# Clustered attention and two dense layers on one core: half-tile PSUM buffers, casts on three engines, a new order

## The chip, the cores and the metric

One core of a Trainium2 chip runs the whole program. The metric is the device time of one execution in microseconds (us). TensorE is called PE below (PEld is its weight load), VectorE DVE, ScalarE ACT, GpSimd POOL and SyncE SP.

## The reference

```
# B, H, S, D = 2, 8, 768, 64; 16 clusters per head
q_assign, k_assign = argmax over the clusters of normalized q, k against normalized centroids
mask   = q_assign[..., :, None] == k_assign[..., None, :]
scores = where(mask, 0.125 * q @ k.T, -1e9)
attn   = exp(scores - max); attn /= sum; x = attn @ v        # 16 heads, (768, 64) each
x = x.transpose(0, 2, 1, 3).reshape(1536, 512)
h = x @ w_in                                                 # 512 -> 2048
x = where(h > 0, h, exp(min(h, 0)) - 1) @ w_out              # 2048 -> 512
out = ((x @ w_a) * (x @ w_b)) @ w_out2                       # 512 -> 1536 -> 512
```

## The kernel before

The program is a list of small operations, written out by hand in the string `ORDER`. A word such as `tr:6.3` calls the operation `tr` with the numbers 6 and 3. No scheduler moves anything: each engine gets its instructions in the order of the words and works them off in that order. Semaphore waits come from the tiles that the instructions share. Two instructions on different engines that touch the same bank of one PSUM tile wait for each other, whichever columns they touch.

**Attention.** The 16 heads go in 8 pairs (pair j holds heads 2j and 2j+1), with 6 tiles of 128 query rows per head, so 12 tiles per pair. For head g and tile t:
- `sc:g.t` (PE): scores into one of two `sc` buffers of two banks. `rm` (DVE) takes the row maximum, and `ex` (ACT) the exponential with its sum, into `pf`. `ex` frees the `sc` buffer.
- The probabilities are needed with keys on partitions, as two 16-bit parts. 30 of the 96 tiles take the way `hi` (cast), `lo` (POOL subtracts), `td` (a transposing DMA). The other 66 take `tr` (six PE transpositions of 128x128 into PSUM), `th` (ACT casts the 768 columns to 16 bits) and `tl` (DVE subtracts that from the 768 columns).
- `av:j.f.n` (PE): the product with v in three parts. `ra`, `rc`, `rx`, `rb`, `re` spread the reciprocals of the sums, `ev` (DVE) scales the result.

Once per pair, ahead of its scores, the clusters are found: `sm` (PE) gives similarities, `sv` copies them out of PSUM, `st` transposes them (PE), `m1` to `m5` are five DVE instructions on the transposed tile in PSUM, `oh` transposes the result back (PE), `ohs` (ACT) scales it, and `ohd` stores it by DMA into rows that the scores use. `lk`, `lq`, `ka1`, `ka2`, `qa`, `qb`, `kbd` load and split a head's k and q; `vs`, `v1`, `v2` do the same for v. At the start `vr` (ACT) takes the maxima of v, which `vtp`, `vtd`, `vbp`, `vbd` spread. `wm` is 8 small matmuls that keep PE busy and whose result nobody reads.

**PSUM in attention.** Four banks are the two `sc` buffers. One tile `places` has three banks, split into two slots of 768 columns, that is one and a half banks each, which `small` hands out in turn: transpositions, `st`, `oh`, `rb`, `vtp` and `vbp` use them. The middle bank belongs to both slots. The last bank is the tile `sums`: `av` and `sm` in its first 384 columns, `wm` in the rest.

**The dense layers** follow: `h`, `r1`, `r2`, `g`, `gh`, `gl`, `x2`, `xa` and `ab`, `bs`, `pr`, `ph`, `pl`, `o`, `oa`, each product as three matmuls of 512 columns, with the weights prepared by `wl` to `wq` (loads, ACT, DVE, POOL) some pieces ahead.

Of the kernel before, what the change touches and what calls it, by code (L numbers as in the profile page):

```python
# [69 lines left out]
m2:0 wm:29 vr:7 m3:0 wm:30 vr:8 wm:31 m4:0 wm:32 vr:9 m5:0 wm:33 vr:10 oh:0 vr:11 wm:34 ohs:0 wm:35  # L70
wm:36 vr:12 ohd:0 wm:37 ka1:2.2 vr:13 wm:38 vr:14 wm:39 ka2:2.1 vr:15 kbd:2 wm:40 vtp:0 qa:2.1 wm:41
vtd:0 wm:42 ka1:3.2 wm:43 wm:44 ka2:3.1 kbd:3 qa:3.1 vbp:0 wm:45 vbd:0 wm:46 wm:47 qb:2 wm:48 wa:1
sc:0.0 w0:1 sc:0.1 rm:0.0 vs:0 wm:49 vs:1 rm:0.1 ex:0.0 wm:50 wm:51 lk:4.0 w1:1 wm:52 lq:4.0 ex:0.1
w2:1 sc:0.2 w3:1 tr:0.0 wh:1 lk:5.0 w4:1 sc:1.0 th:0.0 ws:1 rm:0.2 tr:0.1 v1:0.1 rm:1.0 th:0.1 wm:53
wq:1 wm:54 tl:0.0 wm:55 ex:0.2 wm:56 v2:0.2 wl:2 tl:0.1 wm:57 ex:1.0 sc:1.1 vs:2 wm:58 qb:3 hi:0.2.1
sc:1.2 v1:1.1 rm:1.1 lo:0.2 tr:1.0 lq:5.0 v1:2.1 sm:1.0 rm:1.2 ex:1.1 v2:1.2 td:0.2 th:1.0 sc:0.3
vs:3 wa:2 tr:1.1 rm:0.3 v2:2.2 sv:1.0.1 wm:59 w0:2 th:1.1 sm:1.1 w1:2 ex:1.2 w2:2 w3:2 wh:2 sc:0.4
w4:2 sv:1.1.1 ws:2 tl:1.0 ra:0.0 ex:0.3 rm:0.4 st:1 wq:2 hi:1.2.1 tl:1.1 sc:0.5 ex:0.4 lo:1.2 wl:3
m1:1 tr:0.3 m2:1 qa:4.1 sc:1.3 rm:0.5 ka1:4.2 td:1.2 th:0.3 rc:0.0 ka2:4.1 ex:0.5 kbd:4 m3:1 m4:1
hi:0.5.1 sc:1.4 m5:1 rx:0.0 rm:1.3 wa:3 oh:1 lo:0.5 ohs:1 tl:0.3 ex:1.3 w0:3 ohd:1 tr:0.4 w1:3  # L80
rb:0.0 th:0.4 w2:3 sc:1.5 w3:3 wh:3 w4:3 td:0.5 re:0.0 ws:3 rm:1.4 av:0.0.0 qa:5.1 ex:1.4 tl:0.4
av:0.0.1 wq:3 rm:1.5 tr:1.3 v1:3.1 lk:6.0 ka1:5.2 sc:2.0 th:1.3 qb:4 kbd:5 av:0.0.2 ex:1.5 rm:2.0
ka2:5.1 lq:6.0 tr:1.4 ra:0.1 hi:1.5.1 sc:2.1 ev:0.0 tl:1.3 th:1.4 lo:1.5 ex:2.0 rm:2.1 v2:3.2 tl:1.4
td:1.5 ex:2.1 sc:2.2 lk:7.0 vs:4 tr:2.0 rm:2.2 sc:3.0 vs:5 th:2.0 rc:0.1 tr:2.1 rm:3.0 rx:0.1 ex:2.2
qb:5 th:2.1 sc:3.1 tl:2.0 ex:3.0 lq:7.0 sm:2.0 rm:3.1 hi:2.2.1 sc:3.2 tl:2.1 sv:2.0.1 lo:2.2 rb:0.1
ex:3.1 rm:3.2 av:0.1.0 re:0.1 td:2.2 ex:3.2 sc:2.3 av:0.1.1 rm:2.3 ra:1.0 hi:3.2.1 sc:2.4 rc:1.0
lo:3.2 tr:3.0 rm:2.4 av:0.1.2 th:3.0 rx:1.0 ex:2.3 tr:3.1 ev:0.1 tl:3.0 sm:2.1 th:3.1 td:3.2 ex:2.4
tl:3.1 sc:2.5 sv:2.1.1 sc:3.3 rm:2.5 ka1:6.2 qa:6.1 st:2 ka2:6.1 rm:3.3 kbd:6 ex:2.5 tr:2.3 m1:2
hi:2.5.1 m2:2 sc:3.4 th:2.3 m3:2 lo:2.5 m4:2 ex:3.3 av:1.0.0 m5:2 tl:2.3 v1:4.1 oh:2 v1:5.1 v2:4.2
sc:3.5 rm:3.4 ohs:2 tr:2.4 ka1:7.2 qa:7.1 rm:3.5 ohd:2 rb:1.0 ka2:7.1 th:2.4 av:1.0.1 re:1.0 tl:2.4  # L90
ex:3.4 av:1.0.2 v2:5.2 td:2.5 lk:8.0 tr:3.3 ex:3.5 ev:1.0 kbd:7 tr:3.4 qb:6 th:3.3 sc:4.0 qb:7
# [975 lines left out]
```

## Time and profile before

| | |
|---|---|
| median of 3 runs | 908.3 us (907.98 to 908.95) |
| profiled execution | 908.33 us |
| its span, first to last instruction | 906.5 us |
| mean granted clock of PE | 0.969 of full speed |
| busy, share of the span | PE 94%, DVE 66%, ACT 47%, POOL 37% |

The time holds 1.8 us that lie outside the span. The shares are averages over two stages that differ: attention, to about 350 us, and the dense layers after it.

### The profile page before, as it was taken

The numbers are of one execution on the slowest core, as the hardware profiler recorded it, in microseconds if no ns is written. First come the engines' busy times: TensorE is split into PE (matmuls) and PEld (weight loads), VectorE is DVE, ScalarE is ACT, GpSimd is POOL, SyncE is SP. The second block draws the span as 40 slices with busy tenths as digits, with TensorE's granted clock in tenths as the row PEclk, the third lists the DMA queues.
The fourth block names the chain that finished last, engine by engine and source line by source line (L and its number), as shares of the span: only waits on it lengthen the run. The fifth ranks groups of instructions, "written<-read, shape, count | busy, mean of one in ns | idle before, by whom it ended". The sixth has DMA issues, their size and how long they took to land.

```text
span 906.5 us, 12080 instructions
## 1 busy us (share of the span) xinstructions
PE 850.3 (94%) x4608; PEld 671.6 (74%) x4608; DVE 595.5 (66%) x791; ACT 428.8 (47%) x707; POOL 333.8 (37%) x274
## 2 busy tenths in 40 slices
PE   8878888798898789999999999999999999999997
PEld 7856665565565567888888888888888888888886
DVE  4567677666665778997767868898436772574222
ACT  4667686676766666526417416534122341232120
POOL 4455534526432333454334343445104441252000
PEclk9979999898987999999999999999999999999999
DMA  9345346254423222222222231222002230120102
GB/s 279 99 90 117 69 101 111 50 117 104 94 53 57 45 60 70 70 93 69 70 70 70 69 90 51 72 90 92 25 1 76 87 94 24 47 93 1 40 8 93
DMA packets 65754, 68.32 MB, mean 75 GB/s; under 512 B 49952, under 2 KB 49952, under 8 KB 65696
## 3 DMA queue, kind: packets, MB, share of 16 engines
q1 hardware_dynamic: 65392, 66.86, 27.7%
q10 hardware_dynamic: 304, 0.69, 0.3%
q8 instruction: 36, 0.59, 0.3%
q14 instruction: 22, 0.18, 0.1%
HBM read 48.27 MB, written 3.15 MB: 57 GB/s over the span
## 4 chain that ended last, share of the span: by engine, by line
PE 83%; DVE 8%; ACT 4%; issue 1%; ACTq 0%; DVEq 0%
PE ab L871 7%; PE ab L872 7%; PE ab L870 7%; PE places L673 6%; PE sc L623 6%; PE h L870 5%; PE h L871 5%; PE h L872 5%; PE x L870 5%; PE x L871 5%; PE x L872 5%; PE sums L730 4%; PE o L872 4%; PE o L870 4%; PE o L871 4%; DVE pt L682 4%
## 5 line engine op out<-in xcount | busy, mean ns | idle before, releaser
L631 DVE TENSOR_REDUCE nm<-sc 128x1 f32<-128x768 f32 x96 | 91.0, 952 | 35.2 <-PE sc L623 34.9
L642 ACT ACTIVATE pf<-sc,nm 128x768 f32<-128x768 f32 x96 | 86.5, 904 | 13.2 <-DVE nm L631 12.1
L682 DVE TENSOR_TENSOR pt<-places,pt 128x768 f16<-128x768 f32 x66 | 62.7, 953 | 29.5 <-ACT pt L677 12.4
L655 POOL TENSOR_TENSOR phl<-pf,phl 128x768 f16<-128x768 f32 x30 | 49.4, 1648 | 86.6 <-ACT phl L650 82.4
L677 ACT CAST pt<-places 128x768 f16<-128x768 f32 x66 | 52.4, 798 | 58.0 <-PE places L673 18.5
L673 PE MATMUL places<-identf,pf 128*128 128x128 f32 x396 | 62.9, 302 | 13.3 <-DVE pt L682 5.8
L972 ACT COPY t0ab<-ab 128x512 f32<-128x512 f32 x36 | 21.1, 586 | 110.6 <-PE ab L872 110.6
L977 DVE TENSOR_TENSOR t1ab<-ab,t0ab 128x512 f32<-128x512 f32 x36 | 24.9, 690 | 72.4 <-ACT t0ab L972 72.3
L623 PE MATMUL sc<-ka,qa 128*128 128x384 f32 x192 | 61.8, 405 | 10.9 <-ACT pf L642 10.6
L673 PEld LDWEIGHTS places<-identf,pf 128*128 128x128 f32 x396 | 48.2, 152 | 29.4 <-DVE pt L682 11.2
L730 PE MATMUL sums<-pt,v 128*64 128x384 f16 x576 | 55.0, 333 | 0.0
L623 PE MATMUL sc<-kb,qb 80*128 80x384 f32 x192 | 52.8, 358 | 0.0
L836 DVE SCALAR_TENSOR_TENSOR wg<-wraw,wg 128x512 f32<-128x512 uint32 x68 | 51.2, 754 | 2.0
L623 PEld LDWEIGHTS sc<-ka,qa 128*128 128x128 f32 x192 | 31.8, 204 | 26.4 <-ACT pf L642 18.0
L823 DVE SCALAR_TENSOR_TENSOR wf<-wraw,wg 128x512 int32<-128x512 int32 x68 | 47.0, 691 | 2.0
L806 ACT ACTIVATE wg<-wraw 128x512 f32<-128x512 f32 x68 | 45.3, 669 | 2.3 <-DMA wraw<-in_w_out_dram 2.2
L988 DVE TENSOR_TENSOR gl<-t1ab,gh 128x512 fp32r<-128x512 f32 x36 | 31.5, 874 | 19.9 <-ACT gh L983 19.7
L811 DVE TENSOR_SCALAR wg<-wg 128x512 f32<-128x512 f32 x68 | 44.0, 647 | 0.4
L730 PEld LDWEIGHTS <-v 128*64 128x64 f16 x576 | 29.7, 111 | 19.5 <-issue 7.9
L816 DVE TENSOR_SCALAR wg<-wg 128x512 int32<-128x512 int32 x68 | 40.7, 598 | 2.0
L926 DVE SCALAR_TENSOR_TENSOR t1h<-t0h,h 128x1024 f32<-128x1024 f32 x24 | 29.2, 1217 | 18.6 <-ACT t0h L921 18.6
L831 DVE TENSOR_SCALAR wg<-wf 128x512 int32<-128x512 int32 x68 | 29.0, 427 | 14.9 <-POOL wf L850 13.2
(378 smaller groups left out, 2352.5 us busy)
## 6 DMA issues: line engine op xcount, KB each, us to landing
wraw<-in_w_out_dram SPq DMA_DIRECT2D x28, 512.0 KB, 3.2
wraw<-in_w_in_dram SPq DMA_DIRECT2D x16, 512.0 KB, 3.6
wraw<-in_w_a_dram SPq DMA_DIRECT2D x12, 512.0 KB, 3.5
wraw<-in_w_b_dram SPq DMA_DIRECT2D x12, 512.0 KB, 3.5
rawq<-in_qt_dram SPq DMA_DIRECT2D x30, 192.0 KB, 4.1
acc<-in_v_dram SPq DMA_DIRECT2D x4, 768.0 KB, 10.7
rawk<-in_kt_dram SPq DMA_DIRECT2D x15, 192.0 KB, 3.7
kb<-ka SPq DMA_DIRECT2D x14, 192.0 KB, 3.2
```

Of the source, the lines that this page charges most:

```text
L623: nc.tensor.matmul(s[:, j, :HALF], a[:, qs], b[:, j * HALF : (j + 1) * HALF], start=i == 0, stop=i == 1,)
L631: nc.vector.reduce_max(out=nm, in_=st[g][f"sc{t}"][:, :, :HALF], axis=AX.XY, negate=True)
L642: nc.scalar.activation(pf.rearrange("p (a b) -> p a b", a=2), st[g].pop(f"sc{t}")[:, :, :HALF], AF.Exp, bias=st[g].pop(f"nm{t}"), accum_ou ...
L655: nc.gpsimd.tensor_sub(phl[:, S:], st[g].pop(f"pf{t}"), phl[:, :S])
L673: nc.tensor.transpose(tt[:, ks], pf[:, ks], identf)
L677: nc.scalar.copy(next(parts_of(g, t)), st[g][f"tt{t}"])
L682: nc.vector.tensor_sub(lo, st[g].pop(f"tt{t}"), hi)
L730: nc.tensor.matmul(pairs[j]["av"][x * 64 : (x + 1) * 64].rearrange("p (a q) -> p a q", a=3), st[2 * j + x][("v1", "v2")[vi]][:, kt_, :], s ...
L836: nc.vector.scalar_tensor_tensor(out=g, in0=raws.pop(n)[:, :, 0].bitcast(U32), scalar=2.0 ** -52, in1=g, op0=ALU.mult, op1=ALU.mult,)
L870: nc.tensor.matmul(ps, lhi, rhi, start=first, stop=False)
L871: nc.tensor.matmul(ps, lhi, rlo, start=False, stop=False)
L872: nc.tensor.matmul(ps, llo, rhi, start=False, stop=last)
```

## The change

- `places` and `sums` go. `small` now takes one of three buffers of one bank each (tag `tt`), for half tiles of transpositions and all the small products, `sm` among them. `av` has a bank of its own, which `wm` uses ahead of it.
- `tr`, `th` and `tl` work on half tiles of 384 columns: 132 of each, with three transpositions in a `tr`, where there were 66 with six.
- The result of `m5` and its transposition `oh` are bf16, with a bf16 identity (`ib` makes it).
- Casts and copies that were on one engine are shared out. `hi`: 30 on ACT become 14 on ACT and 16 on POOL. `th`: 66 on ACT become 126 halves on ACT and 6 on DVE. `v1`: 16 on ACT become 5 on DVE, 3 on ACT, 8 on POOL. `v2`: 5 of 16 go from POOL to DVE. `ka1`: 10 of 16 go from POOL to ACT. `qa`: 7 of 15 go from ACT to POOL and 1 to DVE. `re`: 4 of 16 and `sv`: 4 of 16 go from ACT to DVE.
- `ORDER` is a new list; the other operations are the same in number.

```diff
-    places = psumA.tile([P, 2 * S], F32, name="places")
-    nplace = [0]
-    sums = psumA.tile([P, 512], F32, name="sums")
-    def small(shape):
-        o = nplace[0] % 2 * S
-        nplace[0] += 1
-        t = places[: shape[0], o : o + int(np.prod(shape[1:]))]
...
+    def small(shape, name, dt=F32):
+        return take(psumA, "tt", shape, dt, name, 3)
...
-        ps = pairs[j]["sm", hf] = sums[:64, :HALF]
+        ps = pairs[j]["sm", hf] = small([64, HALF], f"sm_{j}_{hf}")
...
-        o = pairs[j]["op"] = small([64, S])
+        o = pairs[j]["op"] = small([64, S], f"op_{j}", BF16)
...
-        (nc.vector.tensor_copy, nc.scalar.copy)[e](phl[:, :S], st[g][f"pf{t}"])
+        (nc.vector.tensor_copy, nc.scalar.copy, nc.gpsimd.tensor_copy)[e](
+            phl[:, :S], st[g][f"pf{t}"]
+        )
...
-        for k in range(NT):
-            ks = slice(k * P, (k + 1) * P)
-            nc.tensor.transpose(tt[:, ks], pf[:, ks], identf)
+    def tr(g, t, u):
+        tt = st[g][f"tt{t}{u}"] = small([P, HALF], f"tt{t}{u}_{g}")
+        pf = st[g][f"pf{t}"]
+        for k in range(3):
+            o = u * HALF + k * P
+            nc.tensor.transpose(tt[:, k * P : (k + 1) * P], pf[:, o : o + P], identf)
...
-            pairs[j]["av"] = sums[:, :HALF]
+            pairs[j]["av"] = take(psumA, "av", [P, HALF], F32, f"av_{j}_{f}")
```

How the new list moves instructions is seen on each engine's own list.

**PE around the cluster step of pair 4, before.** `places` here is first the transposed similarities, then a tile of probabilities, then `oh`.

```order
L557 MATMUL places_82<-identf_88,sim_4_1948 128x64 x6
L623 MATMUL sc4_7_2121<-ka_7_1446,qa_7_1448 128x384 x2
L623 MATMUL sc4_7_2121<-kb_7_1504,qb_7_1521 128x384 x2
L673 MATMUL places_82<-identf_88,pf3_6_2054 128x128 x6
L598 MATMUL places_82<-identf_88,oht_4_2146 64x128 x6
```

The same place now: `tp_4` is the transposed similarities, `op_4` the result of `oh`, `rbp` that of `rb`, `tt30` and `tt31` two half tiles.

```order
L701 MATMUL tt30_6_2252<-identf_87,pf3_6_2223 128x128 x3
L701 MATMUL tt31_6_2259<-identf_87,pf3_6_2223 128x128 x3
L649 MATMUL sc3_7_2263<-ka_7_1586,qa_7_1590 128x384 x2
L649 MATMUL sc3_7_2263<-kb_7_1593,qb_7_1611 128x384 x2
L583 MATMUL tp_4_2273<-identf_87,sim_4_2113 128x64 x6
L741 MATMUL rbp_3_0_2285<-identf_87,rx_3_0_2249 128x128 x3
L649 MATMUL sc4_7_2295<-ka_7_1586,qa_7_1590 128x384 x2
L649 MATMUL sc4_7_2295<-kb_7_1593,qb_7_1611 128x384 x2
L649 MATMUL sc5_7_2313<-ka_7_1586,qa_7_1590 128x384 x2
L649 MATMUL sc5_7_2313<-kb_7_1593,qb_7_1611 128x384 x2
L624 LDWEIGHTS oht_4_2309
L624 MATMUL op_4_2323<-identb_82,oht_4_2309 64x128
```

The tile of probabilities stands ahead of the step instead of inside it, and `rb` and two score tiles stand between `st` and `oh`, where there were one score tile and the tile of probabilities.

**DVE at the same step, before.**

```order
L631 TENSOR_REDUCE nm3_7_2114<-sc3_7_2095 128x1
L570 TENSOR_REDUCE mx_4_2128<-places_82 128x24
L575 TENSOR_TENSOR places_82<-places_82,mx_4_2128 128x384
L580 TENSOR_TENSOR places_82<-places_82,desc_93 128x384
L584 TENSOR_REDUCE mx_4_2128<-places_82 128x24
L589 TENSOR_TENSOR oht_4_2146<-places_82,mx_4_2128 128x384
L682 TENSOR_TENSOR pt1_6_2142<-places_82,pt1_6_2142 128x768
L631 TENSOR_REDUCE nm4_7_2166<-sc4_7_2121 128x1
```

And now:

```order
L710 TENSOR_TENSOR pt1_6_2268<-tt30_6_2252,pt1_6_2268 128x384
L657 TENSOR_REDUCE nm3_7_2280<-sc3_7_2263 128x1
L596 TENSOR_REDUCE mx_4_2291<-tp_4_2273 128x24
L601 TENSOR_TENSOR tp_4_2273<-tp_4_2273,mx_4_2291 128x384
L606 TENSOR_TENSOR tp_4_2273<-tp_4_2273,desc_92 128x384
L610 TENSOR_REDUCE mx_4_2291<-tp_4_2273 128x24
L615 TENSOR_TENSOR oht_4_2309<-tp_4_2273,mx_4_2291 128x384
L710 TENSOR_TENSOR pt1_6_2268<-tt31_6_2259,pt1_6_2268 128x384
L657 TENSOR_REDUCE nm4_7_2321<-sc4_7_2295 128x1
```

The five instructions stay together in this pair; a `tl` on 384 columns stands on either side, where one on 768 stood behind them.

**ACT at the start, before.** `junk,vmax` are the maxima of v (`vr`), `sim_0` the two copies `sv` of pair 0, `ohs_0` its `ohs`.

```order
L549 COPY sim_0_396<-sums_83 64x384
L844 CAST w0h_348<-wf0_351 128x512
L403 ACTIVATE junk_110,vmax_107<-acc_66 128x384 x2
L549 COPY sim_0_396<-sums_83 64x384
L403 ACTIVATE junk_110,vmax_107<-acc_66 128x384 x10
L603 ACTIVATE ohs_0_540<-places_82,ohscale_95 64x768
L403 ACTIVATE junk_110,vmax_107<-acc_66 128x384
L611 DMA kb_0_293<-ohs_0_540 16x768
L611 DMA kb_1_313<-ohs_0_540 16x768
L403 ACTIVATE junk_110,vmax_107<-acc_66 128x384 x3
```

And now:

```order
L519 CAST ka_0_314<-rawk_0_154 64x768
L427 ACTIVATE junk_110,vmax_107<-acc_66 128x384 x14
L629 ACTIVATE ohs_0_541<-op_0_526,ohscale_94 64x768
L836 ACTIVATE wg0_561<-wraw0_250 128x512
L637 DMA kb_0_296<-ohs_0_541 16x768
L637 DMA kb_1_209<-ohs_0_541 16x768
L427 ACTIVATE junk_110,vmax_107<-acc_66 128x384 x2
```

The two copies of similarities have left ACT, so nothing that PE computes stands ahead of the first 14 maxima. On PE `vbp` now stands behind the first two score tiles instead of ahead of them.

## Rows read from the trace of the kernel before

**Rows 1.** The page's slices: TensorE's granted clock, tenths, 40 slices of the span.

```profile
PEclk9979999898987999999999999999999999999999
```

**Rows 2.** Stretches: length, then busy us of PE, PEld, DVE, ACT, POOL; clock, DMA.

```profile
200.00:250.00 50.00, 40.90 (x277) 28.36 (x275) 34.79 (x45) 34.63 (x65) 24.73 (x21) 0.92 0.48 96
...
350.00:400.00 50.00, 50.00 (x220) 40.83 (x219) 45.91 (x53) 24.12 (x31) 20.25 (x13) 1.00 0.22 74
```

**Rows 3.** Timeline around pair 4's cluster step: start, duration, engine, line, [idle before <-releaser].

```profile
169.51 0.58 PE L557 MATMUL places<-identf,sim 64*128 64x64 f32 x6
...
171.69 0.87 PE L673 MATMUL places<-identf,pf 128*128 128x128 f32 x6 [0.64 <-DVE places L575]
...
172.61 0.57 DVE L580 TENSOR_TENSOR places<-places,desc 128x384 f32<-128x384 f32 x1 [0.97 <-PE places L673]
173.21 0.80 ACT L677 CAST pt<-places 128x768 f16<-128x768 f32 x1 [1.49 <-DVE places L580]
...
175.10 0.95 DVE L682 TENSOR_TENSOR pt<-places,pt 128x768 f16<-128x768 f32 x1
...
176.11 1.49 PE L598 MATMUL places<-identf,oht 128*64 128x128 f32 x6 [3.54 <-DVE pt L682]
...
178.68 1.54 PE L673 MATMUL places<-identf,pf 128*128 128x128 f32 x6
...
179.20 1.81 POOL L502 TENSOR_TENSOR ka<-rawk,ka 64x768 fp32r<-64x768 f32 x1
...
179.79 2.03 DVE L456 SCALAR_TENSOR_TENSOR qb<-rawq,qa 64x768 fp32r<-64x768 f32 x1
```

**Rows 4.** Stretches from `oh` to `oh`, and from the last to attention's end.

```profile
176.11:213.02 36.91, 31.79 (x209) 22.39 (x209) 25.45 (x32) 25.55 (x47) 16.69 (x14) 0.92 0.46 91
213.02:250.24 37.22, 32.05 (x209) 22.63 (x209) 25.44 (x32) 25.55 (x47) 16.68 (x14) 0.91 0.49 105
...
287.40:349.60 62.20, 52.50 (x353) 39.51 (x353) 46.09 (x56) 40.77 (x69) 17.55 (x12) 0.93 0.22 52
```

**Rows 5.** DVE by line, 176.11 to 250.24 us: count, busy us, mean ns, idle before.

```profile
L631 DVE TENSOR_REDUCE nm<-sc 128x1 f32<-128x768 f32 x25 | 23.8, 953 | 10.2 <-PE sc L623 10.2
L682 DVE TENSOR_TENSOR pt<-places,pt 128x768 f16<-128x768 f32 x16 | 15.3, 954 | 6.2 <-ACT pt L677 3.5 <-ACT rb L718 1.4 <-PE places L673 1.1
L456 DVE SCALAR_TENSOR_TENSOR qb<-rawq,qa 64x768 fp32r<-64x768 f32 x4 | 5.9, 1485 | 0.0
L740 DVE SCALAR_TENSOR_TENSOR acc<-sums,vback,rb 128x384 f32<-128x384 f32 x4 | 2.5, 618 | 3.0 <-PE sums L730 3.0
...
L575 DVE TENSOR_TENSOR places<-places,mx 128x384 f32<-128x384 f32 x2 | 1.1, 566 | 0.1
```

**Rows 6.** ACT by line, the same stretch.

```profile
L677 ACT CAST pt<-places 128x768 f16<-128x768 f32 x16 | 12.8, 798 | 13.6 <-DVE pt L682 5.3 <-PE places L713 3.9 <-DVE places L580 3.0
L650 ACT CAST phl<-pf 128x768 f16<-128x768 f32 x8 | 6.6, 828 | 0.1
...
L718 ACT COPY rb<-places 128x384 f32<-128x384 f32 x4 | 1.9, 482 | 0.9 <-PE places L713 0.9
```

**Rows 7.** POOL by line, 0 to 500 us.

```profile
L502 POOL TENSOR_TENSOR ka<-rawk,ka 64x768 fp32r<-64x768 f32 x15 | 27.2, 1813 | 2.5 <-DVE ka L495 1.3
...
L495 POOL CAST ka<-rawk 64x768 fp32r<-64x768 f32 x14 | 12.2, 871 | 18.7 <-PE sc L623 17.2 <-DMA rawk<-in_kt_dram 1.4
```

**Rows 8.** ACT in order of time, the start.

```profile
16.16 0.47 ACT L549 COPY sim<-sums 64x384 f32<-64x384 f32 x1 [5.30 <-PE sums L543]
...
20.16 0.47 ACT L549 COPY sim<-sums 64x384 f32<-64x384 f32 x1 [1.84 <-PE sums L381]
```

**Rows 9.** The chain that ended last, the start: start, us, what.

```profile
31.79 0.28 PE places L410
...
34.19 1.89 PE sums L381 x32
36.08 1.46 PE sc L623 x8
```

More of the change, by code (lines that the diff above doesn't have):

```diff
@@ L70 @@
[L70 to L91, printed above, removed]
@@ new lines @@
+c4:0 ka2:1.2 wm:29 wm:33 kb:0 wm:35 wm:34 ka1:0.1 qb:0 wm:30 lk:3.0 wm:41 ka2:0.0 wm:10 lq:2.0 wm:46
+wm:45 qa:1.2 lk:2.0 wm:47 vr:2 wm:25 qb:1 wm:26 vr:0 wm:56 vr:3 lq:3.0 sm:0.0 vr:1 sm:0.1 sv:0.0.0
+vr:5 vr:4 vr:6 wm:22 sv:0.1.0 vr:7 wm:16 st:0 vr:10 wm:38 vr:11 m1:0 wm:20 vr:8 m2:0 wm:40 vr:9 m3:0
+wm:57 wm:42 m4:0 wm:48 m5:0 vr:15 wm:31 vr:13 oh:0 wm:55 ohs:0 wm:4 wm:50 wa:0 ohd:0 wm:53 ka1:3.0
+wm:39 vr:12 w0:0 wm:27 vr:14 w1:0 wm:17 kbd:3 w2:0 qa:2.1 vtp:0 wm:43 w3:0 wm:21 wh:0 w4:0 wm:37
@@ new lines @@
+ka1:2.1 wm:52 vtd:0 ws:0 wm:58 qa:3.1 kbd:2 sc:0.0 wq:0 sc:0.1 rm:0.0 vbp:0 wm:24 rm:0.1 ka2:2.2
+ex:0.0 wl:1 wm:7 wm:36 vbd:0 wm:6 ex:0.1 tr:0.0.0 qb:3 tr:0.0.1 th:0.0.0.1 sc:0.2 th:0.0.1.1 qb:2
+tr:0.1.0 sc:1.0 th:0.1.0.1 rm:0.2 vs:0 lq:4.0 wm:1 vs:2 wa:1 rm:1.0 wm:44 lq:5.0 wm:23 ex:0.2
+ka2:3.2 wm:32 tl:0.0.0 wm:9 tl:0.1.0 hi:0.2.1 tr:0.1.1 tl:0.0.1 sc:1.1 vs:3 ex:1.0 lk:4.0 sm:1.0
+rm:1.1 lk:5.0 lo:0.2 th:0.1.1.1 ex:1.1 tl:0.1.1 tr:1.0.0 sc:1.2 w0:1 td:0.2 th:1.0.0.1 w1:1 tr:1.0.1
+sv:1.0.1 sc:0.3 rm:1.2 v1:0.2 th:1.0.1.1 v2:0.2 tr:1.1.0 tl:1.0.1 ex:1.2 wm:59 vs:1 rm:0.3 wm:49
@@ L338, in c3 @@
     def c3(_):
-        box["cps"] = small([P, P])
+        box["cps"] = small([P, P], "cps")
         nc.tensor.transpose(box["cps"], cn2.rearrange("p a b -> p (a b)"), identf)
@@ L360, in md, with ib @@
     @op
+    def ib(_):
+        nc.vector.tensor_copy(identb, identf)
+    @op
     def md(_):
@@ L375, in sb @@
         nc.gpsimd.memset(ohscale[32:64, 1:2], 0.0)
+    warm_ps = take(psumA, "av", [P, 512], F32, "warm_ps")
     @op
@@ L380, in wm @@
         for _ in range(8):
-            nc.tensor.matmul(sums[:, HALF:], warm[:, :P], warm[:, :P], start=True, stop=True)
+            nc.tensor.matmul(warm_ps[:, :P], warm[:, :P], warm[:, :P], start=True, stop=True)
     def staged(g):
@@ L408, in vtp @@
     def vtp(_):
-        box["vps"] = small([NH, P])
+        box["vps"] = small([NH, P], "vps")
         nc.tensor.transpose(box["vps"], vmax, identf)
@@ L432, in vbp @@
     def vbp(_):
-        vbc = box["vbc"] = small([P, 2, NH])
+        vbc = box["vbc"] = small([P, 2, NH], "vbc")
         nc.tensor.matmul(
@@ L554, in st_ @@
     def st_(j):
-        tp = pairs[j]["tp"] = small([P, NT, 64])
+        tp = pairs[j]["tp"] = small([P, NT, 64], f"tp_{j}")
         for t in range(NT):
@@ L587, in m5 @@
     def m5(j):
-        o = pairs[j]["oht"] = take(ep, "oht", [P, NT, 64], F32, f"oht_{j}", 2)
+        o = pairs[j]["oht"] = take(ep, "oht", [P, NT, 64], BF16, f"oht_{j}", 2)
         nc.vector.tensor_tensor(
@@ L710, in rb @@
     def rb(j, f):
-        p = pairs[j]["rbp", f] = small([P, 3, P])
+        p = pairs[j]["rbp", f] = small([P, 3, P], f"rbp_{j}_{f}")
         for a in range(3):
```

347 lines of the change are left out of this document (192 added, 155 removed).

## The prediction

> **What bounds the kernel now.** The first view is the page's line of TensorE's granted clock [rows 1]: full speed from the middle of the span on, dips only in its first two fifths. The windows say the same in time [rows 2]: from 350 us PE is busy for all of 50 us at clock 1.00, in attention for 40.9 of 50 at 0.92. The dense layers are bound by PE, and none of their operations changes. So time can only come from attention, up to about 350 us, where in that window no engine is busy for more than 41 of 50 us: what limits is who waits for whom.
>
> The second view is the timeline of one such wait [rows 3]. At 169.51 `st` writes one slot of `places`. The next tile's six transpositions go to the other slot, yet PE idles 0.64 us for the DVE instruction `m2` on the first. Then `m3` idles 0.97 us for those transpositions, ACT's `th` 1.49 us for `m3`, and `tl` comes after that. `oh` starts at 176.11, after 3.54 us of idle PE for this `tl`. The slots take turns although they hold different data: both lie on the middle bank. [...]
>
> The third view cuts the span from `oh` to `oh` [rows 4]: a pair takes 36.9 and 37.2 us, 37.05 on average, with PE busy 31.9, DVE 25.45, ACT 25.55, POOL 16.7. PE idles 5.1 us per pair, 3.5 of it ahead of `oh`. Behind that idle the clock is at its lower level: six transpositions take 1.54 us at 178.68 and 0.87 at 171.69 [rows 3]. `oh` itself (1.49), one score tile and one tile of transpositions run so; I put the excess at 0.5 us each, 1.5 per pair.
>
> **The change, step by step.**
>
> *Banks.* Three buffers of one bank each share nothing. What goes per pair on PE: 3.5 us ahead of `oh`, 0.6 ahead of the transpositions, 1.5 of clock. PE alone would then come to 37.05 - 5.6 = 31.4 us. DVE is idle for 11.6 us of a pair (37.05 less 25.45). Of that, `nm` for scores is 10.2 / 2 = 5.1, `pt` for `th`, `re` and transpositions 3.1, `ev` for `av` 1.5 [rows 5]; the rest lies at `m1` to `m5` and in small gaps. The 3.1 and the rest come from shared slots. The 5.1 has to do with the two score buffers, which stay, and I keep it whole; half of `ev`'s 1.5 I keep.
>
> *Half tiles.* A `tl` on 768 columns takes 954 ns; a DVE instruction on 384 columns of PSUM 566 [rows 5]. Per pair 16 x 0.566 - 8 x 0.954 = +1.4 us on DVE. On ACT 798 ns against 482 [rows 6]: nearly 16 x 0.482 - 8 x 0.798 = +1.3, less the few that go to DVE. By the rows, halving costs 0.17 us per tile on either engine. [...]
>
> *Work moved to DVE.* `v1` 5, `v2` 5, `re` 4, `sv` 4, `th` 6, `qa` 1: 25 instructions in 8 pairs, 3.1 per pair. None of the PSUM ones costs more than 0.57 by the row of 384 columns; those in SBUF may cost half. So 0.9 to 1.8 us per pair; I take 1.5, nearer the row. DVE comes to 25.45 + 1.4 + 1.5 = 28.35 us per pair.
>
> *Work moved to and from ACT and POOL.* ACT loses two `hi` of 0.828 per pair [rows 6] and, on balance, more casts than it gets; it ends at or below 25.5. POOL gets two `hi` per pair, one `v1` and 0.9 `qa`, and loses 1.25 `ka1` and 0.6 `v2`. A one-input cast on POOL takes 871 ns, a two-input subtraction 1813 [rows 7]; `qa` there was not seen, so 0.87 to 1.81. POOL gains between 1.5 and 3 us and stays near 19 of 37. I cost this at nothing because POOL has half its time free. What is queued behind a late `hi` on POOL is `lo`, then SP's transposing DMA, and behind that on SP the loads of later heads; `av` needs the result only a dozen score tiles later. Without that cover, each late result would add its delay to an `av`.
>
> *bf16 in `oh`.* Bounds: nothing, or all of a full-clock `oh`, half of 1.49. I take nothing.
>
> *The order at the cluster step.* Between `st` and `oh` PE had one score tile and one tile of transpositions. Now it has `rb` and two score tiles in pair 4, and ten pieces, `av` among them, in pairs 3, 5 and 6. DVE still needs its five instructions there (5 x 0.566 = 2.8 us), with one to ten others between. So some wait at `oh` stays in pairs 1, 2, 4 and 7; that is in what I keep below.
>
> *Sum of a pair.* DVE is now the engine with the longest list of work and waits: 28.35 busy + 5.1 for scores + 0.75 for `av` = 34.2 us. PE alone would allow 31.4. I take the longer, 34.2, so 2.85 us less per pair. From the `oh` at 63 us to that at 287.4 lie 224 us, 6.05 such pairs: -17 us.
>
> *Start.* ACT idles 5.30 us ahead of the first `sv` and 1.84 ahead of the second, this one for `wm`, which shares the bank of `sums` [rows 8]. The 16 maxima stand behind them on ACT, `vtp` waits for the maxima (31.79), and the first scores stand behind it, behind two groups of `wm` and behind `vbp` (36.08) [rows 9]. Now `sv` of pair 0 is on DVE and `vbp` behind the scores. Removed are at most 7.1 on ACT and 4.3 less the `wm` that now stand there; the loads of v and the cluster chain may end later than ACT. Bounds 0 and -8; I take -5, nearer the idle that ACT shows.
>
> *End of attention.* PE idles 62.2 - 52.5 = 9.7 us from the last `oh` on [rows 4]. I take a third, -3 (bounds +2 and -6), since waits for scores and the final weights stay.
>
> Sum: -17 - 5 - 3 = -25. The profiled execution took 908.3 us, its span 906.5, the rest 1.8. The span becomes 881.5 and the time 883.3, so **883 us**. The median before is 908.3 too, so the two compare directly.
>
> **Rivals.**
>
> *PE becomes the bound.* Score waits shrink with the others, because scores wait for `ex`, which waits behind `th` on ACT (13.6 us idle in two pairs [rows 6]). A pair then takes the 31.4 us that PE allows: -5.65 x 6.05 = -34, start -8, end -5: 861 us. For it: PE has no other wait of weight. Against: DVE would be busy 28.35 of 31.4.
>
> *The waits move.* A buffer that holds the transposed similarities from `st` to `m5` leaves two half tiles, one tile's worth, to `tr`; instructions in fixed queues still wait, for a slot or a half of `th` ahead. Per pair only the clock and a little idle go, 36.5 us; start -5: about 900. For it: the short lists in pairs 1, 2, 4, 7.
>
> *Slower: DVE's longer list pays in full.* If DVE's idle comes from the order of the queues and not from banks, its added work lengthens each pair: 25.45 + 2.9 + 11.6 = 39.95, +2.9 x 6.05 = +17.5, less 5 at the start: 921 us. It decides where more than 8.7 of the 11.6 us idle remain. `qb` makes it worse: it took 2.03 us beside a POOL subtraction and 1.485 on average [rows 3, 5], so more work on POOL stretches it. [...] Against this rival: the two groups that grow, `tl` and `nm`, read PSUM and have means of 954 and 953 ns for all POOL's work.
>
> **How the numbers follow.** Forecast 0.53 (its own range 872 to 897), PE the bound 0.13, waits move 0.20, slower 0.14. What a measurement of this kernel tells from no change is about 0.2%, or 1.8 us. Of the third case 0.03 falls within that, the rest is faster: faster 0.83, same 0.03, slower 0.14. The range goes from the second case, 861, to the end of the third, 905; what is left out is the slower case and a little at the lower end.
>
> **What the changed profile would show.** Right: from `oh` to `oh` 34 us; the idle ahead of `oh` under 1.5 us on average; no wait of a transposition for `m2`, nor of `th` for `m3`; the clock in attention at 0.95 or above; DVE near 28 us per pair; the first scores near 31 us. The dense layers as long as before, PE without a gap. Wrong, if `nm` waits more than 5 us per pair for scores, if PE waits on a `tl` for one of the three buffers as often as before, if `av` waits for a transposing DMA, or if DVE's idle stays above 8.7 us per pair.

## The result, and the profile after

The changed kernel takes 866.7 us (median of 4 runs, 863.0 to 868.6) against 908.1 (4 runs, 907.5 to 909.0) for the kernel before: ratio 0.9538, 95% interval 0.9501 to 0.9575. The forecast was 883 us, with a range of 861 to 905: the time lies inside the range, below the 872 to 897 of the likeliest case. The profiled execution took 868.19 us, its span 866.4, that is 40.1 less than the span of before.

Four stretches give the 40.1 us, cut at the first and last `oh` and at the last `ev` (62.90, 287.40 and 349.73 us before; 57.08, 254.52 and 312.22 now): start 62.90 to 57.08, -5.8; six pairs 224.50 to 197.44, -27.1; end of attention 62.33 to 57.70, -4.6; dense layers 556.77 to 554.18, -2.6. The windows of the last three, columns as in [rows 2]:

```profile
57.08:254.52 197.44, 177.66 (x1237) 131.92 (x1236) 165.43 (x264) 138.54 (x295) 120.69 (x99) 0.93 0.50 101
254.52:312.22 57.70, 54.45 (x374) 42.79 (x375) 50.09 (x81) 43.24 (x85) 20.93 (x17) 0.94 0.25 59
312.22:866.40 554.18, 549.62 (x2389) 447.94 (x2388) 354.20 (x470) 191.12 (x267) 179.65 (x122) 1.00 0.20 63
```

A pair now takes 197.44 / 6 = 32.9 us, where it took 224.5 / 6 = 37.4; the two pairs in [rows 4] took 36.9 and 37.2. PE is idle for 3.3 us of it (5.5 before, by the same windows), DVE for 5.3 (11.9 before). PE's own work is shorter too, 29.6 us against 31.9. Part of it is `oh`: all of the six pairs take 3.4 us in bf16 where they took 8.3.

The page's slices of the granted clock, to hold beside [rows 1]; the dips in the first two fifths are fewer, not gone:

```profile
PEclk9998999998898999999999999999999999999999
```

The timeline of pair 4's cluster step, beside [rows 3]. Lines of PE, DVE and ACT from `st` to `oh`:

```profile
152.46 0.58 PE L583 MATMUL tp<-identf,sim 64*128 64x64 f32 x6
...
152.97 0.94 PE L741 MATMUL rbp<-identf,rx 128*128 128x128 f32 x6
...
153.44 0.55 DVE L596 TENSOR_REDUCE mx<-tp 128x24 f32<-128x384 f32 x1
...
154.02 0.57 DVE L601 TENSOR_TENSOR tp<-tp,mx 128x384 f32<-128x384 f32 x1
...
154.24 0.47 ACT L746 COPY rb<-rbp 128x384 f32<-128x384 f32 x1
...
154.62 0.57 DVE L606 TENSOR_TENSOR tp<-tp,desc 128x384 f32<-128x384 f32 x1
...
155.66 0.61 PE L649 MATMUL sc<-ka,qa 128*128 128x384 f32 x2 [1.06 <-ACT pf L668]
...
155.81 0.56 DVE L615 TENSOR_TENSOR oht<-tp,mx 128x384 bf16<-128x384 f32 x1
...
156.55 0.41 PE L624 MATMUL op<-identb,oht 128*64 128x128 bf16 x4
```

`rbp` is written right behind `st` and copied by ACT while `m2` (154.02) and `m3` work on `tp`, and nobody waits for the other's buffer. `oh` has no idle time of PE ahead of it (3.54 us before, 17.1 in the six pairs; now 0.3). What PE waits for here is `ex`, which frees a score buffer.

PE's waits over the six pairs, before: us in total, times, longest.

```profile
PE places L598 <- DVE pt L682: 17.1, 5, 3.5
PE places L673 <- DVE pt L682: 4.7, 9, 2.1
PE sc L623 <- ACT pf L642: 3.9, 2, 2.1
```

And now:

```profile
PE sc L649 <- ACT pf L668: 7.8, 7, 3.4
PE tt L701 <- DVE pt L710: 6.1, 4, 3.3
PE tt L701 <- ACT pf L668: 3.9, 5, 2.3
```

All waits of PE for a `tl` (`pt` of DVE) fall from 23.0 us to 6.5, those of `rb` (1.2 and 0.4) included. But what is left of them, ahead of transpositions, grew from 4.7 to 6.1 us, and the waits for `ex` (`pf`) grew from 3.9 to 11.7.

DVE by line over the six pairs, to hold beside [rows 5], which cover two pairs:

```profile
L657 DVE TENSOR_REDUCE nm<-sc 128x1 f32<-128x768 f32 x72 | 67.8, 948 | 16.1 <-PE sc L649 15.8
L710 DVE TENSOR_TENSOR pt<-tt,pt 128x384 f16<-128x384 f32 x94 | 48.9, 545 | 4.7 <-ACT pt L705 4.5
L480 DVE SCALAR_TENSOR_TENSOR qb<-rawq,qa 64x768 fp32r<-64x768 f32 x12 | 14.5, 1218 | 5.5 <-POOL qa L543 5.5
L770 DVE SCALAR_TENSOR_TENSOR acc<-av,vback,rb 128x384 f32<-128x384 f32 x11 | 6.7, 610 | 1.4 <-PE av L760 1.3
L492 DVE CAST v<-acc 128x384 f16<-128x384 f32 x5 | 6.1, 1239 | 1.2 <-PE av L760 1.2
```

The wait of `nm` for scores is 2.7 us per pair; before it was 29.2 us in the same stretch, 4.9 per pair:

```profile
L631 DVE TENSOR_REDUCE nm<-sc 128x1 f32<-128x768 f32 x73 | 69.5, 953 | 29.2 <-PE sc L623 29.1
```

A new wait stands beside it: `qb` for `qa`. The timeline of the worst case of it:

```profile
223.50 2.13 POOL L543 TENSOR_SCALAR qa<-rawq 128x768 fp32r<-128x768 f32 x1
...
225.66 0.95 DVE L480 SCALAR_TENSOR_TENSOR qb<-rawq,qa 64x768 fp32r<-64x768 f32 x1 [2.67 <-POOL qa L543]
...
225.71 2.59 POOL L526 TENSOR_TENSOR ka<-rawk,ka 64x768 fp32r<-64x768 f32 x1
...
227.53 0.94 DVE L657 TENSOR_REDUCE nm<-sc 128x1 f32<-128x768 f32 x1
...
228.38 1.64 POOL L683 TENSOR_TENSOR phl<-pf,phl 128x768 f16<-128x768 f32 x1
...
230.05 0.90 ACT L668 ACTIVATE pf<-sc,nm 128x768 f32<-128x768 f32 x1 [2.56 <-POOL phl L683]
...
231.09 0.72 PE L649 MATMUL sc<-ka,qa 128*128 128x384 f32 x2 [3.41 <-ACT pf L668]
```

Read downwards: `qa` sits on GpSimd for 2.13 us, `qb` waits for it and the maxima stand behind `qb`; `ka2` and then `lo` stand behind `qa` on GpSimd; `ex` waits for `lo`, and PE stands 3.41 us for that `ex`.

### The profile page after: what moved, and what is told of

It is laid out like the page before. It is cut to its first block, busy times and chain, and to the rows that moved or that the text cites. A ratio compares the mean times of both kernels' runs of the same rounds, so it can differ in the third digit from the quotient of the medians.

```text
span 866.4 us, 12164 instructions
## 1 busy us (share of the span) xinstructions
PE 833.2 (96%) x4608; PEld 667.4 (77%) x4608; DVE 612.2 (71%) x883; ACT 412.1 (48%) x732; POOL 355.5 (41%) x290
## 3 DMA queue, kind: packets, MB, share of 16 engines
q1 hardware_dynamic: 65392, 66.86, 29.2%
## 4 chain that ended last, share of the span: by engine, by line
PE 85%; DVE 7%; POOL 3%; ACT 2%; issue 1%; DMA 0%; ACTq 0%; DVEq 0%; POOLq 0%
PE ab L900 8%; PE ab L901 8%; PE ab L902 8%; PE sc L649 5%; PE h L900 5%; PE h L901 5%; PE h L902 5%; PE x L900 5%; PE x L901 5%; PE x L902 5%; PE tt L701 4%; PE av L760 4%; PE o L902 4%; PE o L900 4%; PE o L901 4%; PE sm L569 3%
## 5 line engine op out<-in xcount | busy, mean ns | idle before, releaser
L701 PE MATMUL tt<-identf,pf 128*128 128x128 f32 x396 | 65.1, 298 | 14.1 <-DVE pt L710 7.7
L710 DVE TENSOR_TENSOR pt<-tt,pt 128x384 f16<-128x384 f32 x132 | 68.7, 545 | 8.5 <-ACT pt L705 8.2
L701 PEld LDWEIGHTS tt<-identf,pf 128*128 128x128 f32 x396 | 49.6, 152 | 27.2 <-ACT pf L668 12.0
L705 ACT CAST pt<-tt 128x384 f16<-128x384 f32 x126 | 57.0, 478 | 25.2 <-PE tt L701 24.1
L683 POOL TENSOR_TENSOR phl<-pf,phl 128x768 f16<-128x768 f32 x30 | 50.8, 1693 | 39.9 <-ACT phl L676 37.4
L760 PE MATMUL av<-pt,v 128*64 128x384 f16 x576 | 52.8, 329 | 0.0
L1018 DVE TENSOR_TENSOR gl<-t1ab,gh 128x512 fp32r<-128x512 f32 x36 | 38.4, 1065 | 19.9 <-ACT gh L1013 19.9
L866 DVE SCALAR_TENSOR_TENSOR wg<-wraw,wg 128x512 f32<-128x512 uint32 x68 | 47.4, 698 | 2.3
L956 DVE SCALAR_TENSOR_TENSOR t1h<-t0h,h 128x1024 f32<-128x1024 f32 x24 | 29.2, 1215 | 25.2 <-ACT t0h L951 25.1
L971 DVE TENSOR_TENSOR gl<-t1h,gh 128x1024 fp32r<-128x1024 f32 x24 | 36.1, 1504 | 5.4 <-ACT gh L964 5.4
L841 DVE TENSOR_SCALAR wg<-wg 128x512 f32<-128x512 f32 x68 | 38.4, 565 | 2.1 <-ACT wg L836 1.9
L846 DVE TENSOR_SCALAR wg<-wg 128x512 int32<-128x512 int32 x68 | 38.0, 559 | 2.1
```

The costliest lines, as they stand in the source:

```text
L683: nc.gpsimd.tensor_sub(phl[:, S:], st[g].pop(f"pf{t}"), phl[:, :S])
L701: nc.tensor.transpose(tt[:, k * P : (k + 1) * P], pf[:, o : o + P], identf)
L705: (nc.vector.tensor_copy, nc.scalar.copy)[e](next(parts_of(g, t, u)), st[g][f"tt{t}{u}"])
L710: nc.vector.tensor_sub(lo, st[g].pop(f"tt{t}{u}"), hi)
L760: nc.tensor.matmul(pairs[j]["av"][x * 64 : (x + 1) * 64].rearrange("p (a q) -> p a q", a=3), st[2 * j + x][("v1", "v2")[vi]][:, kt_, :], s ...
L866: nc.vector.scalar_tensor_tensor(out=g, in0=raws.pop(n)[:, :, 0].bitcast(U32), scalar=2.0 ** -52, in1=g, op0=ALU.mult, op1=ALU.mult,)
```

## The experiments

The ratios below are each to the kernel before, run beside it on the same chip. The first two take the change apart.

**New buffers alone.** The order and the cast engines of before, with half tiles, three buffers, `av` in its own bank and bf16 in `oh`; 38 words move because no more than three buffers may be taken at a time.

```diff
-tr:0.0
+tr:0.0.0 tr:0.0.1
-th:0.0
+th:0.0.0.1 th:0.0.1.1
```

> The three one-bank buffers, the half tiles, the own bank of av and the bf16 transposition, but the order of before (38 of 2394 words stand a little later, where a buffer was not free) and every cast on the engine of before. Theory BANKS (the time went because instructions on different data no longer wait for a shared bank): most of the 41.5 us come, 870 to 885 us, the idle of TensorE ahead of oh under 1 us per pair. Theory ORDER (the new list of words is what counts): at most 10 us come, 898 to 908, since the lists of each engine still wait for each other as before. Theory CASTS (shared-out casts): likewise 895 to 908.

Measured: 893.7 us (891.3 to 900.4), ratio 0.9843 [0.9799, 0.9887]. That lies between the ranges of the theories: the buffers by themselves are worth some 15 us. The trace (an execution of 900.4 us) shows what they do and what they leave. Over its six pairs (66.56 to 285.04 us, 36.4 each) no `th` waits for a subtraction any more, but PE still waits 7.9 us ahead of `oh` and 15.6 us for a free buffer ahead of transpositions, and the maxima wait longer for scores than before:

```profile
L657 DVE TENSOR_REDUCE nm<-sc 128x1 f32<-128x768 f32 x72 | 68.4, 954 | 48.0 <-PE sc L649 47.5
```

**All casts back.** The changed kernel with `hi`, `th`, `v1`, `v2`, `ka1`, `ka2`, `qa`, `re` and `sv` on the engines of before; the order is the new one.

```diff
-qa:0.2 ... ka1:0.1 ... qa:1.2 ... sv:0.0.0
+qa:0.0 ... ka1:0.0 ... qa:1.1 ... sv:0.0.1
```

> The changed kernel with its order and its banks, but every cast and copy (hi, th, v1, v2, ka1, ka2, qa, re, sv) on the engine of before. BANKS and ORDER: 864 to 874 us, since ScalarE is busy for only 166 of 233 us over the seven pairs and has room for them. CASTS: 885 us or more, with ScalarE ahead of the exponentials as the new wait.

Measured: 859.8 us (858.3 to 862.0), ratio 0.946 [0.9441, 0.9479], below that of the change (0.9538 [0.9501, 0.9575]). So the new order on the new buffers brings 34 us beyond the 15, and sharing out the casts costs about 7. With this order and the casts on their old engines, the maxima wait 18.4 us for scores in the six pairs (56.04 to 245.91 us), where the old order on the same buffers had 48.0:

```profile
L657 DVE TENSOR_REDUCE nm<-sc 128x1 f32<-128x768 f32 x72 | 68.0, 950 | 18.4 <-PE sc L649 18.1
```

**The casts shared out in the old order.** The first run with the cast engines of the change (70 words, the reverse of the edit above).

```diff
-ka1:0.0 ... qa:1.1 ... sv:0.0.1
+ka1:0.1 ... qa:1.2 ... sv:0.0.0
```

> The order of before with the new buffers and with the casts on the engines of the changed kernel; against the run with the new buffers alone (893.7 us) only the engines of the casts differ. If sharing out the casts costs what it cost under the new order (866.7 against 859.8, 7 us), it comes to 901 us, between 897 and 906. If the sharing pays where ACT has the longer waits, as in the old order, it comes to 885 to 891 us.

Measured: 903.1 us (899.0 to 908.7), ratio 0.9944 [0.9918, 0.9969], 1% above the first run. The sharing costs as much under the old order as under the new; it does not pay there either.

**Shared bank or shared tile?** Two runs with the three buffers cut from one tile of three banks, the same buffer for each use in both. In one the third buffer is made of the ends of all three banks, so it shares banks with both others (`+` below); in the other it has the middle bank to itself (`-`).

```diff
-            t = ptile[:, 512 : 512 + HALF].rearrange("p (b c) -> p b c", b=3)
+            t = ptile.rearrange("p (b c) -> p b c", b=3)[:, :, HALF:512]
```

> The changed kernel, same order and casts, its three buffers cut out of one tile of three banks: one buffer in the first bank, one in the last, and the third takes 128 columns at the end of each of the three banks, so that it shares a bank with either other buffer (57 of 132 half tiles and 14 of 16 rb use it). Only the sharing is put back. BANKS: 885 to 905 us, with waits of th, tl and transpositions for instructions on other buffers. ORDER and CASTS: 863 to 872 us, no change from the changed kernel.

> The control of the kernel with shared banks: the same one tile and the same assignment of buffers, but the third buffer lies in the middle bank alone. All theories: 862 to 872 us, as the changed kernel. If it is slower than that, the assignment of buffers and not the sharing makes the difference.

Measured: 973.5 us (970.3 to 975.5) with the shared bank, 973.7 (964.6 to 978.7) without. There is no difference between them, and both are 107 us above the changed kernel, which no theory had: whether banks were shared did not matter here, within one tile. Both also hand the buffers out in another sequence than the change does, so a third run keeps its rotation, with one bank for each buffer, and only takes the three from one tile:

```diff
-        return take(psumA, "tt", shape, dt, name, 3)
+        x = next(SLOTS)
+        o = "ABC".index(x) * 512
+        t = ptile[:, o : o + HALF].rearrange("p (b c) -> p b c", b=3)
```

> The changed kernel, its three buffers cut from one tile of three banks instead of three tiles; each buffer still has a bank of its own, the buffers are handed out in the same rotation, and order and casts are the same. By the reading in the prediction (a shared bank makes the waits), nothing is shared and the time stays at 866 us, within 4. By the rival reading (instructions on different engines wait for each other within one tile, whichever bank they touch), a cast of one half waits for the subtraction of another as before the change, and the time goes up by at least 15 us, toward the 973 us of the two kernels with one tile that were run before.

Measured: 974.0 us (971.1 to 976.5), ratio 1.0727 [1.07, 1.0754]. The edit is the tile alone, and it costs 107 us. ACT's casts of half tiles by line, in the six pairs of the changed kernel and in those of this run (63 to 345 us, 47.0 us each):

```profile
L705 ACT CAST pt<-tt 128x384 f16<-128x384 f32 x89 | 40.1, 479 | 17.9 <-PE tt L701 17.1
```

```profile
L717 ACT CAST pt<-ptile 128x384 f16<-128x384 f32 x88 | 40.9, 479 | 86.1 <-PE ptile L713 36.6 <-PE ptile L581 18.9 <-DVE pt L722 9.1
```

Casts now wait for `sm` (`ptile` of L581) and for subtractions (`pt` of L722), which work on other buffers: the three separate tiles are what frees them. One such place, at a cluster step:

```profile
150.90 0.48 ACT L717 CAST pt<-ptile 128x384 f16<-128x384 f32 x1 [2.12 <-DVE mx L622]
...
151.41 0.56 DVE L627 TENSOR_TENSOR oht<-ptile,mx 128x384 bf16<-128x384 f32 x1 [0.55 <-ACT pt L717]
```

The cast of a half tile waits for `m4` (L622), which reads the transposed similarities, and `m5` (L627), which reads them too, waits for the cast. Each of the two buffers has a bank of its own here. In the window of the six pairs PE is busy for 223 of 282 us, and its granted clock is 0.77 (0.93 in the changed kernel):

```profile
63.14:345.24 282.10, 223.18 (x1236) 155.04 (x1235) 164.25 (x262) 141.66 (x294) 116.17 (x96) 0.77 0.35 71
```

**Which cast costs.** The changed kernel with the `qa` of heads 9 and 12 to 15 on ScalarE; the two of the first pair stay on GpSimd (the expectation says seven; five were moved).

```diff
-qa:9.2 ... qa:12.2 ... qa:13.2 ... qa:14.2 ... qa:15.2
+qa:9.1 ... qa:12.1 ... qa:13.1 ... qa:14.1 ... qa:15.1
```

> The changed kernel with the seven qa of GpSimd back on ScalarE; nothing else moves. Theory: the two-microsecond qa on GpSimd holds up qb on VectorE (5.5 us of waits between 30 and 300 us) and stretches it, and the maxima behind qb make ScalarE wait; without it 3 to 5 us less, 862 to 864 us. Rival: what costs is the load that all moved casts add to VectorE (v1, v2, re, sv, th), and qa hides: within 1.5 us of 866.7.

Measured: 857.2 us (855.2 to 860.1), ratio 0.9444 [0.9422, 0.9466]. More than expected, and no slower than with all casts back: as far as these runs tell, these five words are the whole cost of the sharing under the new order. From the `ev` at 178.8 us (177.4 in this run) to that at 256.6 (244.5) alone it gains 10.7 us, where four of the five stand. Its six pairs:

```profile
56.89:242.45 185.56, 169.72 (x1236) 125.61 (x1235) 164.31 (x264) 141.25 (x300) 107.55 (x94) 0.98 0.52 108
```

30.9 us per pair at clock 0.98. Of the 11.9 us by which the six pairs of this execution (855.2 us) are shorter than those of the changed kernel's (868.2), PE's busy time for the same matmuls is 7.9 (177.66 to 169.72 us, clock 0.93 to 0.98) and its idle time 3.9: more came from the clock than from the waits themselves.

**With the five `v1` of VectorE on ScalarE as well:**

```diff
-v1:6.0 ... v1:10.0 ... v1:11.0
+v1:6.1 ... v1:10.1 ... v1:11.1
```

> As the run before it, and the five v1 on VectorE (1239 ns each) back on ScalarE (513 ns each) as well. Theory: the two slow casts are the whole cost of the sharing, 859 to 861 us, like the run with all casts back. Rival: no difference to the run with qa alone, if each v1 falls where VectorE would wait anyway; then the rest of the 7 us lies with hi on GpSimd or with the small copies.

Measured: 860.0 us (857.8 to 861.7), ratio 0.9471 [0.9452, 0.949], not to be told from the run before it. That `v1` took 1239 ns on VectorE cost nothing that shows in the end; my theory held for `qa` alone.

**Load or dependency?** The five `qa` on ScalarE, and GpSimd does the same multiplication on a buffer that nobody reads.

```diff
+            if e == 3:
+                nc.gpsimd.tensor_scalar_mul(idle, idle.bitcast(F32), SCALE)
```

> The run with five qa moved from GpSimd to ScalarE (857.2 us), and at the same five places GpSimd also does a multiplication of the same shape on a buffer that nobody else reads (plus one fill of that buffer, once). Theory A: what costs is that qb, and the maxima behind it on VectorE, wait for a result that comes 2.1 us after its start; GpSimd's load by itself is free, 856 to 859 us. Theory B: what costs is GpSimd's time, by which lo and the copies behind it come late, or VectorE beside it; 863 to 867 us, as the changed kernel.

Measured: 857.4 us (856.6 to 858.1), ratio 0.9442 [0.9424, 0.9461]. The instructions are there, four of the five at 2.13 us and one at 2.83; three of them:

```profile
182.51 2.13 POOL L546 TENSOR_SCALAR idle<-idle 128x768 fp32r<-128x768 f32 x1
...
187.11 2.83 POOL L546 TENSOR_SCALAR idle<-idle 128x768 fp32r<-128x768 f32 x1
...
208.92 2.13 POOL L546 TENSOR_SCALAR idle<-idle 128x768 fp32r<-128x768 f32 x1
```

and cost nothing (857.4 us with them, 857.2 without): the time that GpSimd spends on them is free. What costs, then, is who waits for the result or stands behind it. Which of the two is not told apart: the dummy waits for no load and no score tile, as `qa` did, and does not bring back the late `lo`. In the six pairs `ex` waits 3.2 us for `lo` in the changed kernel, 1.2 with the five `qa` on ScalarE and 0.5 with the dummies.

**The five `qa` on VectorE:**

```diff
-qa:9.2 ... qa:12.2 ... qa:13.2 ... qa:14.2 ... qa:15.2
+qa:9.0 ... qa:12.0 ... qa:13.0 ... qa:14.0 ... qa:15.0
```

> The changed kernel with the same five qa on VectorE instead of GpSimd. One qa there took 0.55 us in the trace, against 0.84 on ScalarE and 2.13 on GpSimd. Theory: each pair's long engine is VectorE, so 5 x 0.55 = 2.8 us is added to it, less the 5.5 us of waits that go and the contention of qb: 857 to 861 us. Rival: ScalarE is what scores wait for (15 us of waits for ex on TensorE), so qa on VectorE is better than on ScalarE, 853 to 856 us.

Measured: 855.2 us (852.5 to 856.6), ratio 0.9412 [0.9388, 0.9436]. The number is the rival's, but the interval overlaps that of `qa` on ScalarE; which of the two is better stays open.

**The start.** `vbp` ahead of the first score tile again:

```diff
+vbp:0
 sc:0.0
...
-vbp:0
```

> The changed kernel with vbp ahead of the first score tile again, as before the change; sv of the first pair stays on VectorE. The run with all casts back had sv on ScalarE and its first score tile at 30.1 us, earlier than the 31.8 of the changed kernel, so sv does not carry the 4 us. Theory: vbp does; first scores at 33.5 to 36 us and the time 1.5 to 4 us longer, 868 to 871. Rival: it is the new order of the rest of the start; first scores within 0.5 of 31.8 and 866 us.

Measured: 869.2 us (866.8 to 870.8), ratio 0.9568 [0.9543, 0.9592]; the interval overlaps that of the change, the rows tell more. `vtp` and the first scores in the changed kernel:

```profile
29.47 0.28 PE L434 MATMUL vps<-identf,vmax 128*16 128x128 f32 x1 [1.79 <-ACT junk L427]
...
29.58 2.40 PE L405 MATMUL warm_ps<-warm 128*128 128x128 bf16 x40
...
31.79 0.60 PE L649 MATMUL sc<-ka,qa 128*128 128x384 f32 x2
```

and with `vbp` first:

```profile
29.93 0.28 PE L434 MATMUL vps<-identf,vmax 128*16 128x128 f32 x1 [1.95 <-ACT junk L427]
30.04 3.86 PE L405 MATMUL warm_ps<-warm 128*128 128x128 bf16 x40
33.83 0.53 PE L458 MATMUL vbc<-vdg,ones 16*128 16x32 f32 x2
34.28 0.62 PE L649 MATMUL sc<-ka,qa 128*128 128x384 f32 x2
```

From `vtp` to scores it is 2.3 us in the one and 4.35 in the other (36.08 - 31.79 = 4.3 before, [rows 9]). Little of this is `vbp`. The 40 matmuls of `wm` behind `vtp` took 2.40 us in the changed kernel and 3.86 here, behind 1.79 and 1.95 us of idle PE; the granted clock was 1.00 (28 to 32 us) and 0.72 (29 to 35 us). So 1.5 of the 2.0 us are the clock of this one execution, and some 0.5 is left for `vbp`, whose start is 0.45 us ahead of the scores. In the kernel before, 64 matmuls of `wm` stood between `vtp` and the scores:

```profile
31.91 1.95 PE L381 MATMUL sums<-warm 128*128 128x128 bf16 x32
33.79 0.40 PE L434 MATMUL places<-vdg,ones 16*128 16x32 f32 x2
34.12 1.96 PE L381 MATMUL sums<-warm 128*128 128x128 bf16 x32
```

That is 3.91 us against 2.40, at clock 1.00 (31 to 37 us). So of the 4.3 us by which the scores come earlier, 2.3 are an earlier `vtp`, 1.5 are `wm` that stand elsewhere now, and, as an estimate from these rows, some 0.5 are `vbp`.

**The best version.** The five `qa` on VectorE, and all casts up to the first `ev` on the engines of before.

```diff
-qa:0.2 ka2:1.2 ka1:0.1 ... sv:0.0.0 sv:0.1.0
+qa:0.0 ka2:1.0 ka1:0.0 ... sv:0.0.1 sv:0.1.1
```

> The changed kernel with the five later qa on VectorE (855.2 us alone) and, up to the first ev, all casts on the engines of before (sixteen words; sv, v1, re and qa on ScalarE, ka1 on GpSimd). The run with all casts back reached its first ev 1.5 us earlier than the changed kernel (64.1 against 65.6). Theory: that is kept to the end, 853 to 855 us, ratio to before 0.940. Rival: the stretch is later eaten by waits, as PE is not yet the bound there: within 1 us of 855.2 or above.

Measured: 852.6 us (852.3 to 856.6), ratio 0.9395 [0.9373, 0.9418], below both kernels: 14 us less than the change. Its first `ev` stands at 65.7 us, as in the change, so what I wanted to keep from the run with all casts back was not kept; and the interval overlaps that of the run before. Its six pairs take 30.6 us each:

```profile
57.62:241.50 183.88, 169.97 (x1236) 125.38 (x1236) 164.96 (x268) 138.26 (x295) 108.71 (x95) 0.98 0.55 109
```

## Why the prediction was right, and where its sizes were off

**Pair period: right in kind, too small.** Forecast was 34.2 us; it is 32.9, from 37.4 over all six pairs. That is 4.5 less per pair instead of 2.85, and six pairs give 27.1 us instead of 17. By the terms of the sum:
- DVE busy, 28.35 forecast: 165.43 / 6 = 27.6. The half tiles cost 16 x 0.545 - 8 x 0.954 = 1.1 us per pair, not 1.4. The moved work was more than my 1.5, and above its bound of 1.8: `v1` 6.1, `v2` 2.9, `th` 2.7, `re` 2.2, `qa` 1.1 and `sv` 1.1 us in six pairs, 2.7 per pair. Of those in SBUF, which I said may cost half, `qa` took 0.55 us on 768 columns, where a `tl` on 768 in PSUM had taken 0.95; on 384 columns `v2` took 0.59 and `v1` 1.24 on average. `qb` gave 0.3 back. By line the busy times grew by 2.9 us per pair (160.7 to 178.1 us in six pairs), but the records of DVE instructions that follow one another overlap, by 12.7 us now and 7.5 before, and only 2.0 per pair show as busy time.
- Score waits, "I keep it whole", 5.1: they are 2.7. **This is the mis-sized term**, and not for the reason that the first rival gave (`ex` behind a `th` that waits). PE's waits for `ex` were 3.9 us in six pairs before and are 11.7 now. And when the new buffers freed `th` in the old order, the wait of the maxima rose from 29.2 to 48.0 us in six pairs; only the new order on the new buffers brought it down, to 18.4 with the old casts and 16.1 in the changed kernel. Which of its moves did so is open.
- Waits of `ev`: 1.4 / 6 = 0.2, not 0.75. In their place stand `qb` for `qa`, 0.9, and `tl` for `th`, 0.8, and small ones. Idle in all: 5.3 per pair, by luck near the 5.85 I had.

**"PE alone would allow 31.4" was too high.** With five `qa` off GpSimd a pair takes 30.9 us, with PE busy for 28.3. I had taken nothing for bf16 in `oh`. At granted clock 1.00 one `oh` takes 0.52 us in bf16 (57.08 to 57.60 us) and took 0.85 before (at 103.77 us; clock 1.00 from 103.5 to 104.8), so bf16 gives some 0.33 per pair, 2.0 of the 4.9 us in six pairs; the other 2.9 I put down to the clock, which I had counted: the `oh` of 1.49 us ran at 0.50 (176.0 to 177.7 us). The clock in the pairs, 0.98 there instead of 0.93, gives more. The change came out between my first two cases, and the rival's 861 us is what it would have come to, and a little below, without those five words. That is its number and not its mechanism: PE then still idles 2.6 us of each pair.

**The banks: the waits were right, their cause was not.** I put them on the middle bank that both slots share. In [rows 3] both slots lie in one tile as well, and the trace cannot tell the two apart. The runs with one tile can: without any shared bank, casts and subtractions on different buffers still wait for each other, and the casts of half tiles idle 86.1 us in the six pairs where on three tiles they idle 17.9. So the description of the kernel before, which has the instructions on one bank of a tile wait for each other, is too narrow: those on different banks of one tile do too, as the cast that waits 2.12 us for `m4`. What took the waits away is that there are three tiles. Whether separate tiles could share a bank was not tried.

**The new order was under-weighed.** I gave it no term of its own beside the wait that stays ahead of `oh` in four pairs. The runs give it 34 of 49 us, once it stands on separate tiles; on one tile with its half tiles, the same order, with the casts shared out, is 65 us slower than before. The buffers alone are worth 15, and the order needs them. What the half tiles, the third buffer and the own bank of `av` each give within the 15 was not taken apart.

**"I cost this at nothing because POOL has half its time free".** Load was free, as the dummy `qa` show. But `qa` was put at 0.87 to 1.81 us and takes 2.13, and `qb` on VectorE, the longest engine, needs it at once. I named `hi` and `lo` as what is queued behind; I did not look at who waits for `qa`. The five `qa` on GpSimd cost 9 us, by the wait of `qb`, the late `lo` behind them, or both.

**Start.** Forecast -5; scores come 4.3 us earlier, the first `oh` behind them 5.8. The working was mostly wrong. `vbp` gives some 0.5, the `wm` that stand elsewhere 1.5, and an earlier `vtp` 2.3. `sv` on VectorE is not shown to be the reason for the last: ACT still idles, 4.97 us, only later, ahead of `ohs` (5.30 and 1.84 before, [rows 8]). ACT's timeline in the changed kernel:

```profile
24.55 0.99 ACT L629 ACTIVATE ohs<-op,ohscale 64x768 f32<-64x768 bf16 x1 [4.97 <-PE op L624]
```

and with `sv` back on ScalarE, among the other casts, `vtp` comes at 27.77, earlier than 29.47. What brought `vtp` 2.3 us forward was not taken apart.

**End of attention** -4.6 (forecast -3, bounds +2 and -6). **Dense layers** -2.6, where I had none; PE is busy 2.6 us less there, and why was not followed.

**The signs.** Right: no idle time ahead of `oh`, no transposition that waits for `m2`, no cast that waits for `m3`, DVE at 28, first scores near 31; of the signs of being wrong, none came: PE waits on a `tl` 5 times in six pairs, 18 before, and `av` waits for nothing. Wrong: the clock in the pairs is 0.93, not 0.95. The slower rival is refuted: DVE's idle fell from 11.9 to 5.3 us, far under its 8.7. So is the case that the waits only move (36.5 us per pair), though in part they did: transpositions wait longer for `tl` than before, 6.1 us against 4.7.

## What to carry to other kernels

When a wait is between instructions that use different data, ask first what the program tracks (here the tile, not the bank): cutting buffers into tiles of their own took away waits that the new order on one tile kept (974.0 us on one tile, 866.7 on three), and the order paid only then. When work is moved to an idle engine, its load need not be the price (here it was not); look at who needs its result, and what stands behind it. A wait that you mean to keep in a sum deserves the question of what feeds it: the score waits grew when the other waits went in the old order, and fell by nearly half with the new one. And before a difference is put down to one moved instruction, look at the granted clock in both traces: with `vbp` first, 1.5 of the 2.0 us were the clock.
